# Casts of the first x ahead of its softmax, W1 in pairs of chunks over four PSUM banks, zero matmuls in the first softmax

## The chip, the cores and the metric

The kernel runs on one core of a Trainium2 chip. The metric is the device time of one execution in microseconds (us). Three runs of the kernel before took 282.36, 283.07 and 284.10 us. The engines are named as in the profile: PE is TensorE's matmul side and PEld its weight loads, DVE is VectorE, ACT is ScalarE, POOL is GpSimd, SP is SyncE, which here only issues DMAs.

## What is computed

The program is a cross attention between a sequence and a small state, followed by a two-layer network with SiLU. There are B = 8 blocks, H = 8 heads, S = 512 positions, Ns = 32 state rows, D = 64.

```
scores  = scale * x @ state^T             # per block and head: 512 x 32
a       = exp(scores) / sum over the 32 state rows
xread   = a @ state                       # 512 x 64
a2      = exp(scores^T) / sum over the 512 positions
sread   = a2 @ x                          # 32 x 64
tokens  = [xread; sread], heads side by side   # 8 * 544 rows of 512
h       = tokens @ w_in                   # 512 -> 2048
out     = (h * sigmoid(h)) @ w_out        # 2048 -> 512, float32
```

The reference subtracts the row maximum in each softmax; the kernel does not.

## The kernel before, in words

**The weights of a block.** For a block, `xread @ w_in` is `a @ (state @ w_in)`. So the kernel first makes `W1 = state @ w_in`, with the state laid out block-diagonally in `sbd`, and then multiplies it by the softmax `a`. W1 has four chunks of 512 columns. `w1_m` (line 231) computes one chunk with 8 matmuls of 64 rows by 32 columns into a pair of PSUM banks, `w1_e` (line 244) casts both banks to bf16 into the tile `W1`, and `W1x` (line 358) does the two for one chunk.

**The steps of a block.** `load_x` and `cast_x` (line 106) bring in x and cast it to bf16. `st_T` (115) transposes the state, `x_T` and `x_Te` (125, 132) transpose x and copy it out of PSUM, `sc` (136) makes the scores, `ex` (148) the exponentials on ACT. `norm_s` (158) sums rows and takes reciprocals on DVE, `norm_m` (163) multiplies, on POOL or DVE, and gives `an`. `a_T` (175) transposes `an` into PSUM and copies it to `aT`. `sread_m`, `sread_n`, `sread_t` (186, 211, 221) make the state read and put its transpose into `xsT`. `g1` (250) is the first layer for one of 16 tiles of 128 hidden columns: two matmuls into bank `h0` or `h1`, in turn, and a SiLU on ACT. `g2` (276) is one matmul of the second layer, `o_e` (295) copies a finished tile of 128 rows of output out of PSUM on DVE and stores it.

**The stages.** The first softmax (lines 331 to 343) takes the four 128-row pairs of heads of block 0 one after the other. Block 0's layers follow, with block 1's attention between them (lines 377 to 442). Then comes a transition (445 to 475). From line 504 on the work is in *phases*: `phase(k, fill)` (477) runs the 64 `g2` steps of block k (four output tiles of 16 steps, banks `o0` and `o1` in turn), and after a step it runs what `fill` lists for that step: the rest of the attention of block n = k + 1, its W1 and its `g1`, and the first part of the attention of block k + 2. `phase(1, ...)` runs only tiles 2 and 3, that is steps 32 to 63. Phases 2 to 6 come from one loop (514 to 528). Phase 7 and the state rows (`g_s`) end the program.

**What sets the order.** The schedule is manual: each engine runs its instructions in the order in which the program writes them, and semaphores are waited for where tiles or PSUM banks demand it. So a wait holds up all that is behind it on that engine. PSUM has eight banks: `o0`, `o1`, `w0`, `w1`, `h0`, `h1`, `a0`, `a1`. ACT loads one function table at a time, for exp or for SiLU; a load is an instruction of its own. `warm` (302) issues zero matmuls. `gate` (93) holds back a load of x by a small write of DVE.

Of the kernel before, what the change touches and what calls it, by code (L numbers as in the profile page):

```python
# [19 lines left out]
def kernel(  # L20
# [53 lines left out]
    def bf(name):  # L74
        return bank[name][:].bitcast(BF16)
# [30 lines left out]
    def cast_x(b, eng, kts=(0, 1, 2, 3)):  # L106
        for kt in kts:
            for h in range(2):
                cp(
                    eng,  # L110
                    x_n[b % 2][:, kt, :, h, :],
                    x_f[b % 2][:, kt, h, :].rearrange("p (c d) -> p c d", c=4),
                )

    def st_T(b, bk, e0, e1):
        v = bf(bk)[:, 0:128]
        nc.tensor.transpose(v, st_nat[:, b, :], ident[:])  # L117
        for half, e in ((0, e0), (1, e1)):
            cp(
                e,  # L120
                sbd[ds(64 * half, 64), b, :, half, :],
                v[ds(64 * half, 64)].rearrange("p (ns kt) -> p kt ns", kt=KT),
            )
# [12 lines left out]
    def sc(b, kt, bk):  # L136
        v = bank[bk][:].rearrange("p (k c e) -> p k c e", k=2, c=4)
        for c in range(4):
            nc.tensor.matmul(  # L139
                v[:, kt % 2, c, :],  # L140
                xT[b % 2][:, kt, c, :],
                sbd[:, b, kt, :, :],
                start=True,
                stop=True,
                skip_group_check=True,
            )

    def ex(b, kt, n, bk):
        v = bank[bk][:].rearrange("p (k q s) -> p k q s", k=2, q=8)
        nc.scalar.activation(  # L150
            en[b % 2][:, :, :, ds(kt, n), :].rearrange("p c h k s -> p k (c h) s"),
            v[:, ds(kt % 2, n)],
            func=EXP,
            bias=0.0,
            scale=SCALE,
        )
# [18 lines left out]
    def a_T(b, bks):  # L175
        n = 2 // len(bks)
        for i, (bk, e) in enumerate(bks):
            v = bf(bk).rearrange("p (h c t) -> p h c t", h=2, c=4)
            for half in range(n):
                for c in range(4):  # L180
                    nc.tensor.transpose(  # L181
                        v[:, half, c, :], an[b % 2][:, c, i * n + half, :, :], ident[:]
                    )
            cp(e, aT[b % 2][:, ds(i * n, n)], v[:, ds(0, n)])

    def sread_m(b, bk):
        v = bank[bk]
        for half in range(2):
            for c in range(4):
                for kt in range(KT):  # L190
                    nc.tensor.matmul(  # L191
                        v[ds(32 * kt, 32), ds(D * half, D)],
                        en[b % 2][:, c, half, kt, :],
                        x_n[b % 2][:, kt, c, half, :],
                        start=(c == 0),
                        stop=(c == 3),
                        skip_group_check=True,
                        tile_position=(0, 32 * kt),
                    )
        for half in range(2):  # L200
            for c in range(4):
                nc.tensor.matmul(
                    v[:, ds(128 + half, 1)],
                    en[b % 2][:, c, half, :, :],
                    ones[:],
                    start=(c == 0),
                    stop=(c == 3),
                    skip_group_check=True,
                )

    def sread_n(b, bk):
        v = bank[bk]
        nc.vector.reciprocal(srec[:], v[:, 128:130])
        nc.vector.tensor_tensor(
            sr[:],
            v[:, 0:128].rearrange("p (h d) -> p h d", h=2),
            srec[:].unsqueeze(2).to_broadcast([128, 2, D]),
            op=MULT,
        )
# [30 lines left out]
    def g1(b, ft):  # L250
        bk = bank[f"h{hctr[0] % 2}"]
        hctr[0] += 1
        if b < B:
            for half in range(2):
                nc.tensor.matmul(  # L255
                    bk[:],
                    W1[b % 2][:, half, ds(128 * ft, 128)],
                    aT[b % 2][:, half, :, :],
                    start=(half == 0),
                    stop=(half == 1),  # L260
                    skip_group_check=True,
                )
            nc.scalar.activation(g[b % 2][:, ft, :], bk[:], func=SILU, bias=0.0)  # L263
        else:
            for kt in range(KT):
                nc.tensor.matmul(  # L266
                    bk[:, 0:256],
                    w_in_sb[:, kt, ds(128 * ft, 128)],
                    xsT[:, kt, :, :, :],
                    start=(kt == 0),  # L270
                    stop=(kt == KT - 1),
                    skip_group_check=True,
                )
            nc.scalar.activation(g_s[:, ft, :], bk[:, 0:256], func=SILU, bias=0.0)  # L274

    def g2(b, tt, ft, bk, cols=(0, 512)):
        src = g[b % 2] if b < B else g_s
        c0, c1 = cols
        nc.tensor.matmul(  # L279
            bank[bk][:, c0:c1],  # L280
            src[:, ft, ds(128 * tt, 128)],
            w_out_sb[:, ft, c0:c1],
            start=(ft == 0),
            stop=(ft == 15),
            skip_group_check=True,
        )
# [8 lines left out]
    def o_e(b, tt, bk, eng="dve", q=None, cols=(0, 512)):  # L295
        t = o_sb[octr[0] % 4]
        octr[0] += 1
        c0, c1 = cols
        cp(eng, t[:, c0:c1], bank[bk][:, c0:c1])
        (q or nc.sync).dma_start(o_dst(b, tt, c0, c1), t[:, c0:c1])  # L300
# [8 lines left out]
    with tc.manual_schedule():  # L309
# [20 lines left out]

        XB = ("o0", "o1", "w0", "w1")
        SB = ("h0", "h1", "a0", "a1")
        st_T(0, "a1", "act", "dve")
        for i in range(5):
            if i < 4:
                cast_x(0, "dve", (i,))
                x_T(0, i, XB[i])
                x_Te(0, i, 1, XB[i], "act")
            if i > 0:
                sc(0, i - 1, SB[i - 1])  # L340
                ex(0, i - 1, 1, SB[i - 1])
                norm_s(0, i - 1, 1)
                norm_m(0, "dve", i - 1, 1)
        nc.scalar.preload_act_table(SILU)
        a_T(0, (("a0", "dve"), ("a1", "act")))
        w1_m(0, 0, ("w0", "w1"))
        w1_e(0, 0, ("w0", "w1"), ("dve", "act"))
# [10 lines left out]
        def W1x(b, j, bks, engs):  # L358
            w1_m(b, j, bks)
            w1_e(b, j, bks, engs)  # L360

        def exps(b):
            ex(b, 0, 2, "a0")
            ex(b, 2, 2, "a1")
            norm_s(b)
            norm_m(b, "pool")
# [78 lines left out]
        for ft in range(10):  # L445
# [5 lines left out]
            if ft == 7:  # L451
                scs(2, 0)
                scs(2, 1)
        exps(2)
        g1(1, 12)
        g1(1, 13)
        g2(1, 0, 10, "o0")
        g2(1, 0, 11, "o0")
        for ft in range(12):
            g2(1, 1, ft, "o1")  # L460
            if ft % 3 == 1:
                W1x(2, ft // 3, ("w0", "w1"), ("dve", "dve"))
            if ft == 5:
                sread_m(1, "a1")
                sread_n(1, "a1")
            if ft == 10:
                sread_t(1, "a1", "dve")
        cast_x(3, "pool")
        for ft in range(12, 16):
            g2(1, 0, ft, "o0")  # L470
            g2(1, 1, ft, "o1")
            if ft < 14:
                g1(1, ft + 2)
        o_e(1, 0, "o0")
        o_e(1, 1, "o1")

# [9 lines left out]
        def add(fill, step, *fs):  # L486
            fill.setdefault(int(step), []).extend(fs)

        def L(f, *a):
            return lambda: f(*a)  # L490

        def att_tail(fill, b, s_m, s_t, s_a):
            add(fill, s_m, L(sread_m, b, "a1"), L(sread_n, b, "a1"))
            add(fill, s_t, L(sread_t, b, "a1", "dve"))
            add(fill, s_a, L(a_T, b, (("a0", "dve"),)))
# [6 lines left out]
            add(fill, s1 + 2, L(scs, b, 1))  # L502

        fill = {}
        add(fill, 34, L(a_T, 2, (("a0", "dve"),)))
        for i in range(16):
            add(fill, 36 + 1.7 * i, L(g1, 2, i))
        add(fill, 38, L(sread_m, 2, "a1"), L(sread_n, 2, "a1"))
# [2 lines left out]
        phase(1, fill, (2, 3))  # L511


        for k in range(2, 7):
            n = k + 1
            fill = {}
            exps(n)
            if k + 2 < B:
                load_x(k + 2, nc.sync)
                cast_x(k + 2, "pool")  # L520
            for j in range(4):
                add(fill, 3 + 3 * j, L(W1x, n, j, ("w0", "w1"), ("dve", "dve")))
            att_tail(fill, n, 15, 25, 21)
            for i in range(16):
                add(fill, 25 + 2.3 * i, L(g1, n, i))
            if k + 2 < B:
                att_head(fill, k + 2, 42, 56)
            phase(k, fill)


        fill = {}
# [42 lines left out]
```

## Time and profile before

| what | value |
|---|---|
| runs | 282.36, 283.07, 284.10 us |
| profiled execution, its own time | 283.27 us |
| its span | 281.5 us |
| PE busy | 237.8 us (84%) |
| ACT busy | 120.1 us (43%) |
| DVE busy | 103.0 us (37%) |
| POOL busy | 43.8 us (16%) |
| mean DMA rate | 78 GB/s |

The span is the stretch between the first and the last instruction of the profiled execution; 1.77 us of its time lie outside it. An instruction's line is that of the helper that issued it, so most groups are told apart by the tiles they write: `ps_o`, `ps_w`, `ps_h`, `ps_a` are the PSUM banks. "idle before" is the time in which the engine stood still just before a group, with what released it. The busy time of a group of matmuls includes the tail of the last one, so the pace of a stream is read from one start to the next. PEclk is the clock granted to TensorE, as a share of 2.4 GHz.

### The profile page before, as it was taken

What the parts mean: (1) busy time and instruction counts of PE and PEld (TensorE: products, weight loads), DVE (VectorE), ACT (ScalarE), POOL (GpSimd) and SP (SyncE); (2) the same over time, 40 slices, a digit from 0 to 9 for tenths busy, and PEclk for the clock granted to TensorE, in tenths of its full rate; (3) what the DMA queues carried; (4) which work ended last, traced back from release to release, by engine and by line L of the source; (5) the groups of instructions that cost most, each with busy time, mean ns of one, the idle gap of its engine ahead of it and who ended that gap; (6) DMA issues with size and microseconds to landing.
All of it is one profiled execution on the core that took longest, in us unless ns stands there. A gap on an engine that the chain in (4) does not pass through costs nothing.

```text
span 281.5 us, 4371 instructions
## 1 busy us (share of the span) xinstructions
PE 237.8 (84%) x1777; PEld 112.8 (40%) x1810; DVE 103.0 (37%) x194; ACT 120.1 (43%) x194; POOL 43.8 (16%) x81
## 2 busy tenths in 40 slices
PE   4359979996889778996989778996989698999994
PEld 3223343342245324541435324541445234456643
DVE  3452215725533274226613273225603472000110
ACT  2353574566136604552075504562075505643301
POOL 5631202123300060002300060002300010000000
PEclk9999997999899979997799979998899979999999
DMA  5999800750020231006111231116010001110112
GB/s 170 188 202 204 175 2 0 239 212 1 0 77 37 71 119 40 37 37 186 38 39 40 68 118 40 38 40 186 37 41 37 37 2 45 66 40 37 40 75 76
DMA packets 19828, 22.07 MB, mean 78 GB/s; under 512 B 3040, under 2 KB 15584, under 8 KB 19808
## 3 DMA queue, kind: packets, MB, share of 16 engines
q1 hardware_dynamic: 12576, 16.39, 17.5%
q0 software_dynamic: 6128, 4.42, 10.5%
q10 hardware_dynamic: 1104, 0.98, 1.1%
q8 instruction: 14, 0.23, 0.3%
q14 instruction: 6, 0.05, 0.1%
HBM read 17.30 MB, written 8.91 MB: 93 GB/s over the span
## 4 chain that ended last, share of the span: by engine, by line
PE 71%; ACT 11%; DVE 10%; issue 5%; DMA 1%; ACTq 0%; POOL 0%; DVEq 0%
PE ps_o L279 33%; PE ps_h L255 19%; PE ps_w L234 4%; DVE W L79 3%; DVE rs L160 3%; ACT L150 3%; ACT en L150 3%; PE ps_w L279 3%; PE ps_h L266 2%; ACT g L263 2%; PE ps_a L128 2%; ACT L263 1%; PE ps_a L181 1%; DMA st_f<-in_state_dram 1%; PE ps_a L191 1%
## 5 line engine op out<-in xcount | busy, mean ns | idle before, releaser
L279 PE MATMUL ps_o<-w_out_sb,g 128*128 128x512 bf16 x458 | 137.4, 395 | 4.1 <-issue 2.2
L263 ACT ACTIVATE g<-ps_h 128x512 bf16<-128x512 f32 x128 | 75.4, 597 | 60.3 <-PE ps_h L255 56.5
L255 PE MATMUL ps_h<-aT,W 128*128 128x512 bf16 x246 | 74.8, 387 | 5.6 <-ACT g L263 3.6
L279 PEld LDWEIGHTS <-g 128*128 128x128 bf16 x512 | 47.6, 100 | 58.2 <-issue 14.8
L79 DVE COPY o_sb<-ps_o 128x512 f32<-128x512 f32 x30 | 20.5, 688 | 72.7 <-PE ps_o L279 72.7
L255 PEld LDWEIGHTS <-W 128*128 128x128 bf16 x256 | 24.7, 99 | 33.8 <-issue 7.7
L165 POOL TENSOR_TENSOR an<-en,rs 128x1024 bf16<-128x1024 bf16 x7 | 13.4, 1911 | 144.8 <-DVE rs L161 144.8
L79 DVE CAST W<-ps_w 128x512 bf16<-128x512 f32 x49 | 31.2, 678 | 12.5 <-PE ps_w L234 12.5
L263 ACT ACT_TABLE_LOAD x7 | 9.0, 1283 | 60.7 <-PE ps_h L255 60.6
L234 PE MATMUL ps_w<-w_in_sb,sbd 64*32 64x512 bf16 x200 | 17.6, 488 | 16.8 <-DVE W L79 16.6
L81 POOL CAST x_n<-x_f 128x256 bf16<-128x256 f32 x52 | 18.5, 407 | 25.1 <-DMA x_f<-in_x_dram 13.5
L234 PEld LDWEIGHTS <-sbd 64*32 64x32 bf16 x256 | 5.9, 92 | 39.5 <-issue 39.3
L160 DVE TENSOR_REDUCE rs<-en 128x32 f32<-128x1024 bf16 (+1 forms) x11 | 10.2, 929 | 25.0 <-ACT en L150 25.0
L128 PEld LDWEIGHTS <-x_n 128*128 128x128 bf16 x128 | 8.7, 102 | 9.4 <-DVE x_n L79 6.4
L79 DVE COPY xT<-ps_a 128x1024 bf16<-128x1024 bf16 x13 | 8.9, 691 | 9.5 <-PE ps_a L128 9.5
L79 DVE COPY sbd<-ps_a 64x128 bf16<-64x128 bf16 x15 | 4.3, 288 | 19.8 <-PE ps_a L117 16.8
L274 ACT ACTIVATE g_s<-ps_h 128x256 bf16<-128x256 f32 x16 | 6.1, 384 | 11.8 <-PE ps_h L266 11.8
L279 PE MATMUL ps_w<-w_out_sb,g 128*128 128x512 bf16 x31 | 10.2, 412 | 0.1
L266 PE MATMUL ps_h<-xsT,w_in_sb 128*128 128x256 bf16 x64 | 9.6, 273 | 0.0
L150 ACT ACT_TABLE_LOAD x7 | 9.0, 1283 | 0.1
L150 ACT ACTIVATE en<-ps_a 128x512 bf16<-128x512 f32 (+1 forms) x16 | 8.4, 568 | 0.3 <-PE ps_a L139 0.2
L128 PE MATMUL ps_a<-ident,x_n 128*128 128x128 bf16 x112 | 8.3, 219 | 0.0
(56 smaller groups left out, 122.7 us busy)
## 6 DMA issues: line engine op xcount, KB each, us to landing
out_dram<-o_sb SPq DMA_DIRECT2D x32, 256.0 KB, 2.3
x_f<-in_x_dram SPq DMA_DIRECT2D x7, 1024.0 KB, 6.4
w_in_sb<-in_moe_w_in_dram POOLq DMA_DIRECT2D x4, 512.0 KB, 11.4
w_out_sb<-in_moe_w_out_dram POOLq DMA_DIRECT2D x4, 512.0 KB, 13.2
x_f<-in_x_dram SPq DMA_DIRECT2D x2, 256.0 KB, 3.2
x_f<-in_x_dram ACTq DMA_DIRECT2D x2, 256.0 KB, 4.0
out_dram<-o_sb ACTq DMA_DIRECT2D x1, 256.0 KB, 2.5
st_nat<-in_state_dram POOLq DMA_DIRECT2D x7, 32.0 KB, 11.1
```

The source lines that it names most:

```text
L79: nc.vector.tensor_copy(dst, src)
L81: nc.gpsimd.tensor_copy(dst, src)
L128: nc.tensor.transpose(v[:, kt % 2, c, :], x_n[b % 2][:, kt, c, :, :], ident[:])
L150: nc.scalar.activation(en[b % 2][:, :, :, ds(kt, n), :].rearrange("p c h k s -> p k (c h) s"), v[:, ds(kt % 2, n)], func=EXP, bias=0.0, sc ...
L160: nc.vector.tensor_reduce(v, en[b % 2][:, :, :, ds(kt, n), :], axis=AX, op=ADD)
L165: e.tensor_tensor(an[b % 2][:, :, :, ds(kt, n), :].rearrange("p c h k s -> p (c h) k s"), en[b % 2][:, :, :, ds(kt, n), :].rearrange("p c ...
L234: nc.tensor.matmul(bank[bks[half]][ds(32 * kt, 32), :], sbd[ds(64 * half, 64), b, kt, half, :], w_in_sb[ds(64 * half, 64), kt, ds(512 * j, ...
L255: nc.tensor.matmul(bk[:], W1[b % 2][:, half, ds(128 * ft, 128)], aT[b % 2][:, half, :, :], start=(half == 0), stop=(half == 1), skip_group ...
L263: nc.scalar.activation(g[b % 2][:, ft, :], bk[:], func=SILU, bias=0.0)
L266: nc.tensor.matmul(bk[:, 0:256], w_in_sb[:, kt, ds(128 * ft, 128)], xsT[:, kt, :, :, :], start=(kt == 0), stop=(kt == KT - 1), skip_group_ ...
L274: nc.scalar.activation(g_s[:, ft, :], bk[:, 0:256], func=SILU, bias=0.0)
L279: nc.tensor.matmul(bank[bk][:, c0:c1], src[:, ft, ds(128 * tt, 128)], w_out_sb[:, ft, c0:c1], start=(ft == 0), stop=(ft == 15), skip_group ...
```

## The change

Four edits. (1) In the first softmax all eight casts of x come ahead of the loop, on DVE; the second of the two copies of the state transpose goes from DVE to ACT; 4, 4 and 14 zero matmuls are added. (2) In the transition the four W1 chunks of block 2 stand at other places, and the row sums and the multiplication (`norm_s`, `norm_m`) behind two of the chunks. (3) In phases 2 to 6 a new function `W1p` makes two chunks at a time, one into `w0`, `w1`, the other into `h0`, `h1`; the first pair stands at the start of the phase, ahead of `norm_s`, the second after step 18. (4) The copy of `aT` for blocks 2 to 7 goes from DVE to ACT, `a_T` stands at step 29 instead of 21, `sread` at 18 and 30 instead of 15 and 25, `g1` at 32 + 1.9 i instead of 25 + 2.3 i, the head of block k + 2 at 40 instead of 42.

```diff
--- before.py
+++ after.py
@@ -330,18 +330,22 @@
 
         XB = ("o0", "o1", "w0", "w1")
         SB = ("h0", "h1", "a0", "a1")
-        st_T(0, "a1", "act", "dve")
+        st_T(0, "a1", "act", "act")
+        warm(4, "h0")
+        cast_x(0, "dve", (0, 1, 2, 3))
         for i in range(5):
             if i < 4:
-                cast_x(0, "dve", (i,))
                 x_T(0, i, XB[i])
                 x_Te(0, i, 1, XB[i], "act")
             if i > 0:
                 sc(0, i - 1, SB[i - 1])
+                if i == 1:
+                    warm(4, "a1")
                 ex(0, i - 1, 1, SB[i - 1])
                 norm_s(0, i - 1, 1)
                 norm_m(0, "dve", i - 1, 1)
         nc.scalar.preload_act_table(SILU)
+        warm(14, "o0")
         a_T(0, (("a0", "dve"), ("a1", "act")))
         w1_m(0, 0, ("w0", "w1"))
         w1_e(0, 0, ("w0", "w1"), ("dve", "act"))
@@ -451,19 +455,24 @@
             if ft == 7:
                 scs(2, 0)
                 scs(2, 1)
-        exps(2)
+        ex(2, 0, 2, "a0")
+        ex(2, 2, 2, "a1")
         g1(1, 12)
         g1(1, 13)
         g2(1, 0, 10, "o0")
+        W1x(2, 0, ("w0", "w1"), ("dve", "dve"))
         g2(1, 0, 11, "o0")
         for ft in range(12):
             g2(1, 1, ft, "o1")
-            if ft % 3 == 1:
-                W1x(2, ft // 3, ("w0", "w1"), ("dve", "dve"))
-            if ft == 5:
+            if ft == 3:
+                W1x(2, 1, ("w0", "w1"), ("dve", "dve"))
+                norm_s(2)
+                norm_m(2, "pool")
                 sread_m(1, "a1")
+            if ft == 8:
                 sread_n(1, "a1")
-            if ft == 10:
+                W1x(2, 2, ("w0", "w1"), ("dve", "dve"))
+            if ft == 11:
                 sread_t(1, "a1", "dve")
         cast_x(3, "pool")
         for ft in range(12, 16):
@@ -471,6 +480,8 @@
             g2(1, 1, ft, "o1")
             if ft < 14:
                 g1(1, ft + 2)
+            if ft == 13:
+                W1x(2, 3, ("w0", "w1"), ("dve", "dve"))
         o_e(1, 0, "o0")
         o_e(1, 1, "o1")
 
@@ -502,7 +513,7 @@
             add(fill, s1 + 2, L(scs, b, 1))
 
         fill = {}
-        add(fill, 34, L(a_T, 2, (("a0", "dve"),)))
+        add(fill, 34, L(a_T, 2, (("a0", "act"),)))
         for i in range(16):
             add(fill, 36 + 1.7 * i, L(g1, 2, i))
         add(fill, 38, L(sread_m, 2, "a1"), L(sread_n, 2, "a1"))
@@ -511,20 +522,32 @@
         phase(1, fill, (2, 3))
 
 
+        WP = (("w0", "w1"), ("h0", "h1"))
+
+        def W1p(b, i):
+            for j in range(2):
+                w1_m(b, 2 * i + j, WP[j])
+            for j in range(2):
+                w1_e(b, 2 * i + j, WP[j], ("dve", "dve"))
+
         for k in range(2, 7):
             n = k + 1
             fill = {}
-            exps(n)
+            ex(n, 0, 2, "a0")
+            ex(n, 2, 2, "a1")
+            W1p(n, 0)
+            norm_s(n)
+            norm_m(n, "pool")
             if k + 2 < B:
                 load_x(k + 2, nc.sync)
                 cast_x(k + 2, "pool")
-            for j in range(4):
-                add(fill, 3 + 3 * j, L(W1x, n, j, ("w0", "w1"), ("dve", "dve")))
-            att_tail(fill, n, 15, 25, 21)
+            add(fill, 18, L(W1p, n, 1), L(sread_m, n, "a1"), L(sread_n, n, "a1"))
+            add(fill, 29, L(a_T, n, (("a0", "act"),)))
+            add(fill, 30, L(sread_t, n, "a1", "dve"))
             for i in range(16):
-                add(fill, 25 + 2.3 * i, L(g1, n, i))
+                add(fill, 32 + 1.9 * i, L(g1, n, i))
             if k + 2 < B:
-                att_head(fill, k + 2, 42, 56)
+                att_head(fill, k + 2, 40, 56)
             phase(k, fill)
 
 
```

Three places show what this does to the order of instructions. The first is DVE at the start of a phase (phase 2, block 3: `W_82` is its W1, `en_74` its exponentials, `rs_78` its row sums, `o_sb` output tiles). A piece of the difference, - before and + now:

```order
+L79 CAST W_82<-ps_w_97 128x512
+L79 CAST W_82<-ps_w_98 128x512
+L79 CAST W_82<-ps_h_99 128x512
+L79 CAST W_82<-ps_h_100 128x512
 L160 TENSOR_REDUCE rs_78<-en_74 128x32
 L161 RECIPROCAL rs_78<-rs_78 128x32
+L79 COPY o_sb_91<-ps_o_95 128x512
 L79 CAST W_82<-ps_w_97 128x512
 L79 CAST W_82<-ps_w_98 128x512
```

The casts of the first two chunks now stand ahead of the row sums, from four banks, and the first output tile of the phase is copied before the second pair of chunks.

The second place is ACT between the exponentials and the first SiLUs of the same block, the kernel as changed (`aT_80` is the transposed softmax, `g_84` the SiLU's output). A piece of the difference:

```order
+L150 ACT_TABLE_LOAD
+L150 ACTIVATE en_74<-ps_a_101 128x2x8x32
+L150 ACTIVATE en_74<-ps_a_102 128x2x8x32
+L83 ACTIVATE aT_80<-ps_a_101 128x1024
 L263 ACT_TABLE_LOAD
 L263 ACTIVATE g_84<-ps_h_99 128x512
```

The copy of `aT` has become the last thing that ACT does before it loads the SiLU table; before, DVE did it.

The third place is DVE in the first softmax (`x_f_67` is x as loaded, `x_n_69` its bf16 form, `an_75` the softmax):

```order
-L79 COPY sbd<-ps_a_102 64x4x32
-L79 CAST x_n_69<-x_f_67 128x4x64 x4
+L79 CAST x_n_69<-x_f_67 128x4x64 x8
 L160 TENSOR_REDUCE rs_77<-en_73 128x8
 L161 RECIPROCAL rs_77<-rs_77 128x8
 L165 TENSOR_TENSOR an_75<-en_73,rs_77 128x8x32
-L79 CAST x_n_69<-x_f_67 128x4x64 x2
```

The casts of the third and fourth pair of heads stood behind the row sums of the first and second; now no cast waits for a row sum.

## Rows read from the trace of the kernel before

**Rows 1.** Page, part 4: the chain that ended last, share of the span by engine.
```profile
PE 71%; ACT 11%; DVE 10%; issue 5%; DMA 1%; ACTq 0%; POOL 0%; DVEq 0%
```

**Rows 2.** Timeline, start of phase 4: start us, us, engine, line, operation [idle before].
```profile
158.99 0.41 PE L234 MATMUL ps_w<-w_in_sb,sbd 64*32 64x512 bf16 x8
159.33 0.82 PE L279 MATMUL ps_o<-w_out_sb,g 128*128 128x512 bf16 x3
...
160.52 1.22 DVE L160 TENSOR_REDUCE rs<-en 128x32 f32<-128x1024 bf16 x1 [1.60 <-ACT en L150]
...
162.05 1.22 DVE L79 CAST W<-ps_w 128x512 bf16<-128x512 f32 x2
162.30 1.91 POOL L165 TENSOR_TENSOR an<-en,rs 128x1024 bf16<-128x1024 bf16 x1 [25.56 <-DVE rs L161]
...
163.32 0.41 PE L234 MATMUL ps_w<-w_in_sb,sbd 64*32 64x512 bf16 x7 [0.22 <-DVE W L79]
```

**Rows 3.** Windows: length, busy (x) PE, PEld, DVE, ACT, POOL, PEclk, DMA, GB/s.
```profile
165.00:167.50 2.50, 2.05 (x17) 0.58 (x17) 1.35 (x3) 0.00 (x0) 1.47 (x5) 0.50 0.01 5
...
250.00:276.00 26.00, 25.84 (x160) 15.71 (x161) 3.46 (x5) 6.74 (x17) 0.00 (x0) 1.00 0.14 51
```

**Rows 4.** Timeline, the rest of phase 4.
```profile
168.66 0.42 PE L191 MATMUL ps_a<-x_n,en 128*32 128x64 bf16 x32
...
169.44 1.24 PE L279 MATMUL ps_o<-w_out_sb,g 128*128 128x512 bf16 x5
...
170.52 0.61 PE L181 MATMUL ps_a<-ident,an 128*128 128x128 bf16 x8
...
170.97 1.03 PE L279 MATMUL ps_o<-w_out_sb,g 128*128 128x512 bf16 x4
171.17 0.69 DVE L79 COPY aT<-ps_a 128x1024 bf16<-128x1024 bf16 x1 [0.67 <-PE ps_a L181]
...
171.91 0.59 PE L255 MATMUL ps_h<-aT,W 128*128 128x512 bf16 x2
...
174.53 0.59 PE L255 MATMUL ps_h<-aT,W 128*128 128x512 bf16 x2 [0.73 <-ACT g L263]
...
188.46 1.89 PE L279 MATMUL ps_o<-w_out_sb,g 128*128 128x512 bf16 x8
```

**Rows 5.** Timeline, an ACT copy of the size of `aT`, in block 0's stage.
```profile
36.92 1.02 ACT L83 ACTIVATE xT<-ps_a 128x1024 bf16<-128x1024 bf16 x1 [0.24 <-PE ps_a L128]
```

**Rows 6.** Timeline, the transition.
```profile
63.99 1.02 PE L279 MATMUL ps_o<-w_out_sb,g 128*128 128x512 bf16 x4
...
76.93 1.29 DVE L79 COPY o_sb<-ps_o 128x512 f32<-128x512 f32 x2 [1.53 <-PE ps_o L279]
...
79.71 1.24 PE L255 MATMUL ps_h<-aT,W 128*128 128x512 bf16 x4 [0.35 <-DVE aT L79]
```

**Rows 7.** Timeline, the first softmax.
```profile
6.10 1.04 PE L128 MATMUL ps_o<-ident,x_n 128*128 128x128 bf16 x8 [1.44 <-DVE x_n L79]
...
10.59 0.60 ACT L83 ACTIVATE xT<-ps_w 128x512 bf16<-128x512 bf16 x1 [2.38 <-PE ps_w L128]
...
13.08 0.61 PE L128 MATMUL ps_w<-ident,x_n 128*128 128x128 bf16 x4 [2.31 <-DVE x_n L79]
...
14.81 0.38 ACT L150 ACTIVATE en<-ps_a 128x256 bf16<-128x256 f32 x1 [0.21 <-PE ps_a L139]
...
16.84 1.03 PE L181 MATMUL ps_a<-ident,an 128*128 128x128 bf16 x8 [2.07 <-DVE an L165]
```

**Rows 8.** Windows of PE alone: length, busy (x), PEclk, DMA share, GB/s.
```profile
28.00:29.00 1.00, 1.00 (x7) 1.00 2.15 150
...
31.00:32.00 1.00, 1.00 (x7) 1.00 1.09 385
```

**Rows 9.** Timeline, block 1's x arrives and is transposed.
```profile
33.61 1.71 DVE L79 CAST x_n<-x_f 128x256 bf16<-128x256 f32 x4 [5.82 <-DMA x_f<-in_x_dram]
...
35.83 1.06 PE L128 MATMUL ps_a<-ident,x_n 128*128 128x128 bf16 x16
```

## The prediction, made before the change was run

> **What bounds the kernel now.** I read the page's chain first: 71% of the span is PE's, 21% ACT's and DVE's [rows 1]. So PE sets the time, except in places where it waits, and the question is where. The timeline answers that, one phase being enough because phases 2 to 6 come from one loop. Phase 4 starts four `g2` steps before its first W1 chunk, at 158.13 (158.99 less 4 x 0.216; five steps take 1.08 from 169.44 to 170.52) [rows 2, 4]. It ends at 189.32, four steps into the row at 188.46 [rows 4]: 31.19 us. The reader is to see two things in it. First, after one chunk and three steps PE stops near 160 and makes its next whole chunk only from 163.32, because `w0`, `w1` are still full: their casts run at 162.05, behind the row sums, which stand ahead of them on DVE and wait for the exponentials [rows 2]. Second, after that wait the granted clock is 0.50, the level of 1.2 GHz, in the stretch from 165.0 to 167.5 [rows 3], so chunks and steps run at half pace. From 163.32 to 168.66 PE does three chunks and nine steps, at full pace 3 x 0.34 + 9 x 0.216 = 2.96 us, in 5.34 [rows 2, 4]: 2.4 us lost to a second wait for casts and to the clock. From 174.53 to the end PE runs without a break.
>
> **The phases (edit 3, with the steps and `aT` of edit 4).** I write out a new phase from its start, with durations of phase 4.
> - A pair of chunks is 2 x 0.34 = 0.68 (158.99 to 159.33 is one) [rows 2]. Nothing holds it: `w0`, `w1` are empty, and the last SiLU on `h1` ends about 0.2 after the phase's start, before the second chunk needs it at 0.34.
> - Steps 0 to 18: 19 x 0.216 = 4.10, so 4.78. The second pair needs the four casts of the first. DVE copies an output tile (0.69, as 1.29 for two) [rows 6], then casts two pairs of banks at 1.22 each [rows 2]: done at about 3.3. No wait. The pair ends at 5.46.
> - `sread_m` 0.78 (168.66 to 169.44) gives 6.24, steps 19 to 29 give 8.62. `a_T` needs `an`: row sums 1.22 and reciprocal from 3.3 to about 4.9, then POOL's 1.91 [rows 2], so 7.0. Slack 1.6.
> - `a_T` 0.45 (170.52 to 170.97) gives 9.07; three steps and the transpose of `sr` give 9.80 [rows 4]. The transpose needs `sr` at 9.29. DVE copies tile 0 (to 5.55), casts four banks (to 8.0) and scales (to 8.5): slack 0.8.
> - `g1` needs `aT`. DVE's copy began 0.65 after the start of `a_T` and took 0.69 [rows 4]; an ACT copy of the same size took 1.02 [rows 5]. So `aT` is there at 8.62 + 0.65 + 1.02 + 0.05 = 10.34, and PE waits **0.54**, which it did not before.
> - From the first `g1` to the third PE takes 2.62 (171.91 to 174.53), bound by ACT's load of the SiLU table, not by PE's own work [rows 4]. That stays: 12.96. One step less than before covers it.
> - The rest took 14.79 with 34 steps (174.53 to 189.32); now 28 are left: 14.79 - 1.30 = 13.49. `g1` comes every 1.9 steps; two matmuls and two steps are 0.86, as in most of the old stretch, so the SiLUs keep up.
>
> The new phase is 26.45, 4.74 less; five of them make **23.7**. Bounds: if both waits behind step 29 vanished in full, a further 0.54 each, 26.4; if the clock falls there (a rival), 10 less.
>
> DMAs: the load of x for block k + 2 is issued from SP where it was, behind the last tile's store. POOL's casts of it stand behind `norm_m`, which ends later in the phase by some 0.9 us, but they are used only at step 42, far behind.
>
> **The transition (edit 2).** From 63.99 to the first `g1` of block 2 at 79.71 is 15.72 [rows 6]. PE's work in it is 27 steps (5.83), four chunks (1.36), two `g1` (0.86), `sread` with its transpose (0.86) and `a_T` (0.45): 9.36. With chunks 0 and 1 cast ahead of the row sums, DVE is busy nearly throughout from 64.6: eight casts in pairs of 1.22 to 1.29, row sums 1.5, the scaling and copy of `sr` 0.9, then the first output tile 0.69 [rows 2, 6], done at about 73.7. The waits left are some 0.3 for the casts of chunk 0, 0.45 for `sr`, 1.2 at step 32 for that tile, and 0.85 for `aT` from ACT: 2.8. So 9.36 + 2.8 = 12.2 and the gain is **3.6**. These waits lie close together; if the clock falls to its lower level there the gain is 1.9 or less. I keep 3.6 and take 1.6 as the lower end.
>
> **The first softmax (edit 1).** The transposes of the fourth pair of heads start at 13.08, having waited for its cast, and `a_T` follows 3.76 later at 16.84 [rows 7]. With all casts ahead, a pair of heads advances at ACT's pace, a copy of 0.60 and an exponential of 0.38 [rows 7]. If the first transposes still start at 6.10, the fourth start at about 6.10 + 3 x 1.0 = 9.1 and `a_T` at 12.8: 4.0 earlier. The second state copy on ACT (0.3 or less, a half of 0.60 by size) precedes the first transposes' copy and hides behind the casts. The zero matmuls cost nothing: at the pace of `a_T`'s eight, 1.03 in all, the last fourteen take 1.8, and PE's idle time ahead of `a_T` is 2.07 [rows 7].
>
> What of the 4.0 reaches the end depends on block 1's x. Its casts start when it lands, at 33.61, and its transposes at 35.83, hardly later than the casts allow [rows 9]. Its load is held back by `gate`, which moves with PE, to a time when more of the weights are still on their way. Beside the weights the two move 150 GB/s together, alone x moves 385 [rows 8]. So the load takes longer: if it gains nothing from its earlier issue, the term is 0; if it shares without loss, 4.0. Nothing in the trace decides; I take **2.0**.
>
> The Trainium skill (DMA: Bandwidth & Descriptors, section "SWDGE vs HWDGE vs iDMA") says that transfers issued from POOL and those from SP use different queues in each DMA engine, and that the engine serves its queues in turn. By that rule x gets about half of the 150 GB/s and lands no earlier than now, so the first softmax would give 0 and the time would be 256.0. The trace agrees so far as the joint rate is the lower one; one such stretch of 1 us is all that it shows.
>
> **The sum.** 2.0 + 3.6 + 23.7 = 29.3. The profiled execution took 283.27, 0.2 above the median of the runs shown, 283.07: 283.27 - 29.3 = **254.0 us**.
>
> **The rivals.**
> - *The clock falls behind step 29* (0.14). The 0.54 for `aT` and the 1.1 or so of the table load now lie within 3.2 us of each other, with 1.5 us of matmuls between. For it: a pause near 160 was followed by 0.50 [rows 3]. Against it: that pause was above 3 us, and the old wait of 0.73 at 174.53 was followed by unbroken work at full pace [rows 4]. Each fall costs at most the 2.4 us found above, say 2.0; in five phases 10: 264.
> - *The pause only moves* (0.05): the change does not do what it says, because the second chunk's bank `h1` comes free only when ACT is through, and the exponentials follow the SiLUs there. If PE waited for them, to about 2.6 after the phase's start, 2.3 would go in each phase: 265.5. Against it: the bank needs only the SiLU, which stands ahead of the table load and the exponentials.
> - *The clock falls and stays down, and the kernel is slower* (0.02). The same place, but TensorE does not come back to 2.4 GHz in the dense rest of the phase. 13.5 us at half clock add 13.5 per phase, 67 in all: 321. It decides from about 12 us at the lower level in each phase (29.3 / 5 is 5.9 us lost). Against it: after the pause of phase 4 the pace was full again by 169.44 [rows 4], and from 250 to 276 PE is busy for 25.84 of 26 us at a clock of 1.00 [rows 3], so density alone lowers nothing.
> - *The chains' slack is used up* (0.05): DVE or POOL runs later than I wrote, so that `sr` or `an` is late. Every 0.5 us beyond the slack of 0.8 or 1.6 costs 2.5 in five phases; 1 us gives 259.
>
> **The numbers.** My forecast has 0.74; the rivals 0.14, 0.05, 0.02 and 0.05. From the sum's bounds: the best is 4.0 + 3.6 + 26.4 = 34.0, 249; the worst without a rival 0 + 1.6 + 23.7 = 25.3, 258. The first rival reaches 264, and the range takes in most of it: 248 to 263. About 1% is what a measurement of this kernel tells from no change. All cases but the third rival are over 1% faster: 0.97 faster, 0.01 within, 0.02 slower.
>
> **What would show it.** In the changed profile the distance from one load of the exp table to the next should be 26 to 27 us in phases 2 to 5; no PE wait near the start of a phase; all eight casts of the W1 pairs without a PE wait on them; a wait of about 0.5 for `aT` from ACT and one of about 1 at the third `g1`; a granted clock of 1.00 throughout phases 2 to 6. Block 1's casts should start between 30 and 33, and the first `g1` of block 2 some 5 to 6 us earlier than 79.71. I am wrong if a 0.50 stretch appears in the phases, if the pause comes back elsewhere, or if the weights' loads become the bound of the first 40 us.

## The result and the profile after

The changed kernel took 254.85 us, the median of four runs (254.44 to 255.27), against 283.13 for the kernel before beside it (282.36 to 284.1): a ratio of 0.900, 95% interval 0.897 to 0.903. The forecast was 254.0 in 248 to 263. The profiled run took 255.27; its span is 253.5, so 1.77 lie outside it, as before. From profiled run to profiled run the change gained 28.0 us, where 29.3 were forecast.

The page of the changed kernel first: span, busy times, the row of the granted clock over 40 slices of 6.3 us, and the chain that ended last.

```profile
span 253.5 us, 4473 instructions
...
PE 226.9 (90%) x1832; PEld 112.4 (44%) x1832; DVE 95.8 (38%) x187; ACT 126.4 (50%) x201; POOL 43.8 (17%) x81
...
PEclk9959989999999999999999999999999999999999
...
PE 77%; ACT 7%; DVE 6%; DMA 6%; issue 3%; ACTq 0%; DVEq 0%
```

PE now carries 77% of the chain where it had 71%, and ACT and DVE 13% where they had 21% [rows 1]. The share of DMA has grown from 1% to 6%, and the clock's row has its low slices near the start alone, in the third and the sixth. Both are taken up below.

To split the gain I take ACT's loads of the exp table, one at the head of every block's exponentials, as marks in both traces.

| from mark to mark | before | after | gain | forecast |
|---|---|---|---|---|
| start to the load at 63.53 / 64.07 | 63.53 | 64.07 | -0.54 | 2.0 |
| from there to 95.01 / 92.36 (transition, phase 1) | 31.48 | 28.29 | 3.19 | 3.6 |
| from there to 220.39 / 197.27 (phases 2 to 5) | 125.38 | 104.91 | 20.47 | 18.96 (4 x 4.74) |
| the rest (phase 6 and the end) | 62.88 | 58.00 | 4.88 | 4.74 |

The last row is the profiled time less the mark. So the phases gave 25.35 (23.7 forecast), the transition nearly its 3.6, and the first softmax cost a little where it should have given 2.0.

**A phase.** The timeline of the changed kernel, phase 2 (start us, us, engine, line, operation, idle before), which answers to [rows 2, 4]:

```profile
92.00 0.41 PE L234 MATMUL ps_w<-w_in_sb,sbd 64*32 64x512 bf16 x8
...
92.23 0.56 PE L234 MATMUL ps_h<-w_in_sb,sbd 64*32 64x512 bf16 x8
92.36 1.28 ACT L150 ACT_TABLE_LOAD   x1
...
92.72 1.28 DVE L79 CAST W<-ps_w 128x512 bf16<-128x512 f32 x2
...
92.73 4.28 PE L279 MATMUL ps_o<-w_out_sb,g 128*128 128x512 bf16 x19
...
93.92 1.28 DVE L79 CAST W<-ps_h 128x512 bf16<-128x512 f32 x2
95.11 1.21 DVE L160 TENSOR_REDUCE rs<-en 128x32 f32<-128x1024 bf16 x1
...
96.93 0.41 PE L234 MATMUL ps_w<-w_in_sb,sbd 64*32 64x512 bf16 x8
...
97.49 0.42 PE L191 MATMUL ps_a<-x_n,en 128*32 128x64 bf16 x32
...
100.42 0.61 PE L181 MATMUL ps_a<-ident,an 128*128 128x128 bf16 x8
...
101.13 1.02 ACT L83 ACTIVATE aT<-ps_a 128x1024 bf16<-128x1024 bf16 x1 [6.39 <-PE ps_a L181]
...
102.20 0.59 PE L255 MATMUL ps_h<-aT,W 128*128 128x512 bf16 x2 [0.47 <-ACT aT L83]
...
102.88 1.28 ACT L263 ACT_TABLE_LOAD   x1 [0.72 <-PE ps_h L255]
...
104.82 0.59 PE L255 MATMUL ps_h<-aT,W 128*128 128x512 bf16 x2 [0.94 <-ACT g L263]
...
118.55 1.28 ACT L150 ACT_TABLE_LOAD   x1
```

The reader is to see that no PE row of the phase before 102.20 carries an idle time. The pair of chunks at 92.00 goes straight into 19 steps, while DVE casts all four banks before it sums the rows. Only the two forecast waits are left: for `aT` at 102.20 and for the SiLU at 104.82. From one exp load to the next are 26.19 us. The clock behind those waits stays at 2.4 GHz, as the windows of the changed kernel show (length, busy (x) of PE, PEclk, DMA share, GB/s); the last row is more than three phases, the others belong to the next two readings and answer to [rows 8]:

```profile
12.00:13.00 1.00, 0.92 (x8) 0.50 1.44 185
21.00:22.00 1.00, 0.78 (x10) 1.00 1.24 207
27.00:28.00 1.00, 1.00 (x13) 1.00 1.15 243
30.00:31.00 1.00, 0.69 (x4) 1.00 1.32 275
32.00:33.00 1.00, 0.00 (x0) 1.00 1.73 136
37.00:38.00 1.00, 1.00 (x3) 0.50 0.00 0
45.00:46.00 1.00, 0.80 (x10) 1.00 0.00 0
118.00:200.00 82.00, 77.76 (x660) 1.00 0.26 81
```

**The start and the transition.** The timeline of the changed kernel there, which answers to [rows 6, 7, 9]:

```profile
9.47 0.94 PE L304 MATMUL ps_o<-zeros 128*128 128x128 bf16 x14
12.08 1.03 PE L181 MATMUL ps_a<-ident,an 128*128 128x128 bf16 x8 [1.66 <-DVE an L165]
...
33.55 1.72 DVE L79 CAST x_n<-x_f 128x256 bf16<-128x256 f32 x4 [11.07 <-DMA x_f<-in_x_dram]
...
34.52 0.40 PE L128 MATMUL ps_a<-ident,x_n 128*128 128x128 bf16 x4 [3.83 <-DVE x_n L79]
...
64.54 0.38 PE L279 MATMUL ps_o<-w_out_sb,g 128*128 128x512 bf16 x1
...
74.63 0.81 PE L279 MATMUL ps_o<-w_out_sb,g 128*128 128x512 bf16 x3 [1.03 <-DVE o_sb L79]
...
77.06 0.59 PE L255 MATMUL ps_h<-aT,W 128*128 128x512 bf16 x2 [0.74 <-ACT aT L83]
```

`a_T` of block 0 starts at 12.08, 4.76 earlier than at 16.84 [rows 7]. But block 1's x is cast from 33.55, where it was 33.61 [rows 9]: its load was released at 22.42 instead of 27.73 and took 11.1 us where it had taken 5.9. PE comes to the transposes of x 3.83 early and waits there, and behind that wait the clock stands at 0.50, the level of 1.2 GHz, from 36 to 39. The transition runs from 64.54 to 77.06, 12.52 us, against 15.72 [rows 6] and a forecast of 12.2.

### The profile page after: what moved, and what is told of

It is laid out like the page before. It is cut to its first block, busy times and chain, and to the rows that moved or that the text cites. A ratio compares the mean times of both kernels' runs of the same rounds, so it can differ in the third digit from the quotient of the medians.

```text
span 253.5 us, 4473 instructions
## 1 busy us (share of the span) xinstructions
PE 226.9 (90%) x1832; PEld 112.4 (44%) x1832; DVE 95.8 (38%) x187; ACT 126.4 (50%) x201; POOL 43.8 (17%) x81
## 4 chain that ended last, share of the span: by engine, by line
PE 77%; ACT 7%; DVE 6%; DMA 6%; issue 3%; ACTq 0%; DVEq 0%
PE ps_o L279 39%; PE ps_h L255 21%; DMA x_f<-in_x_dram 6%; PE ps_h L266 3%; PE ps_a L128 3%; ACT aT L83 2%; PE ps_w L279 2%; PE ps_w L234 2%; ACT g L263 2%; PE ps_a L181 2%; DVE W L79 2%; DVE rs L160 2%; PE ps_a L139 1%; ACT L263 1%; DVE x_n L79 1%
## 5 line engine op out<-in xcount | busy, mean ns | idle before, releaser
L279 PE MATMUL ps_o<-w_out_sb,g 128*128 128x512 bf16 x480 | 133.4, 381 | 1.1 <-DVE o_sb L79 1.0
L255 PE MATMUL ps_h<-aT,W 128*128 128x512 bf16 x256 | 76.8, 385 | 9.5 <-ACT g L263 4.7
L83 ACT ACTIVATE aT<-ps_a 128x1024 bf16<-128x1024 bf16 (+1 forms) x8 | 7.3, 918 | 37.8 <-PE ps_a L181 37.8
L79 DVE CAST W<-ps_w 128x512 bf16<-128x512 f32 x29 | 18.7, 684 | 7.8 <-PE ps_w L234 7.8
L79 DVE CAST W<-ps_h 128x512 bf16<-128x512 f32 x20 | 12.8, 681 | 0.0
L128 PE MATMUL ps_a<-ident,x_n 128*128 128x128 bf16 x112 | 8.9, 225 | 4.2 <-DVE x_n L79 4.2
L79 DVE CAST x_n<-x_f 128x256 bf16<-128x256 f32 x12 | 3.9, 383 | 13.9 <-DMA x_f<-in_x_dram 13.9
## 6 DMA issues: line engine op xcount, KB each, us to landing
out_dram<-o_sb SPq DMA_DIRECT2D x32, 256.0 KB, 2.4
x_f<-in_x_dram SPq DMA_DIRECT2D x2, 256.0 KB, 3.0
x_f<-in_x_dram ACTq DMA_DIRECT2D x2, 256.0 KB, 3.8
out_dram<-o_sb ACTq DMA_DIRECT2D x1, 256.0 KB, 2.5
```

Of the source, the lines that this page charges most:

```text
L79: nc.vector.tensor_copy(dst, src)
L83: nc.scalar.activation(dst, src, func=COPY, bias=0.0)
L128: nc.tensor.transpose(v[:, kt % 2, c, :], x_n[b % 2][:, kt, c, :, :], ident[:])
L255: nc.tensor.matmul(bk[:], W1[b % 2][:, half, ds(128 * ft, 128)], aT[b % 2][:, half, :, :], start=(half == 0), stop=(half == 1), skip_group ...
L279: nc.tensor.matmul(bank[bk][:, c0:c1], src[:, ft, ds(128 * tt, 128)], w_out_sb[:, ft, c0:c1], start=(ft == 0), stop=(ft == 15), skip_group ...
```

## The experiments

Ten kernels were run. "After" is the changed kernel, and each edit is made to it. Ratios are to the kernel before on the same chip, with their 95% intervals; after has 0.900. The medians of the kernel before beside them lie between 282.80 and 284.02 us, so a difference to after in us is good to about 1 us; where the trace has the length of a phase, that is the firmer number. After's phases are 26.23 long on average (104.91 / 4).

**1. The first softmax as before.** Edit 1 is taken back.

```diff
-        st_T(0, "a1", "act", "act")
-        warm(4, "h0")
-        cast_x(0, "dve", (0, 1, 2, 3))
+        st_T(0, "a1", "act", "dve")
         for i in range(5):
             if i < 4:
+                cast_x(0, "dve", (i,))
...
-                if i == 1:
-                    warm(4, "a1")
...
-        warm(14, "o0")
```

> The kernel as changed, but with the first softmax as it was before (casts inside the loop, second state copy on DVE, no zero matmuls). Theory A: up to about 33.5 us the DMAs are the bound, since block 1's x lands at 33.5 whether its load is issued at 22.4 or at 27.8; so edit 1 is worth nothing: 254.3, between 253.8 and 255.4, with the DVE casts of block 1 again starting at 33 to 34 and no PE wait of 3.8 us in front of them. Rival B: edit 1 gave the predicted 2.0 and something else took it back: 256.5 to 257.

256.36 us (254.3 to 256.85), ratio 0.904 (0.900 to 0.908). That lies between the two expectations, and its runs show what it goes with: those with a mean granted clock of 1.00 and 0.993 took 254.3 and 254.77, the four at 0.985 or 0.986 took 256.28 to 256.85. The timeline of this kernel:

```profile
33.67 1.71 DVE L79 CAST x_n<-x_f 128x256 bf16<-128x256 f32 x4 [6.95 <-DMA x_f<-in_x_dram]
```

and, of PE,

```profile
34.77 0.39 PE L128 MATMUL ps_a<-ident,x_n 128*128 128x128 bf16 x4
```

The x lands where it lands in after, with its load released 4.3 us later, and PE arrives at the transposes just in time for it, 0.25 behind after. So nearly all of the 4.8 us that edit 1 gains in front is spent in the wait for x. What is left between the medians, 1.5, goes with the clock later on: the profiled run of this kernel (256.85) loads the exp table for block 1 at 38.89, ahead of after's 40.22, and for block 2 at 65.68, behind after's 64.07. In between it was at 1.2 GHz from 43 to 49.5, where after's was not (its row 45 to 46 above, against this one of PE).

```profile
45.00:46.00 1.00, 1.00 (x10) 0.50 0.00 0
```

**2. Block 1's x loaded early.** Its gate and load stand right behind the casts of block 0.

```diff
         cast_x(0, "dve", (0, 1, 2, 3))
+        gate(1)
+        load_x(1, nc.sync)
...
-        gate(1)
-        load_x(1, nc.sync)
         cast_x(1, "dve", (0, 1))
```

> The kernel as changed, with the gate and the load of block 1's x moved to right behind the casts of block 0's x, so at about 7 us instead of 22.4. Theory A: the wait of 3.8 us ahead of block 1's transposes and the low clock behind it go; PE does not wait for the weights, which land some 3 us later than now but are used later still: 249 to 251. Rival B: the DMAs are the bound through the weights too, so PE waits for w_in or w_out instead of x: 253.5 to 256, with PE or DVE waits on them between 12 and 30 us.

250.50 us (250.06 to 251.22), ratio 0.884 (0.881 to 0.887): 4.4 us less than after, as Theory A had it. The timeline of this kernel, DVE and PE:

```profile
22.70 0.89 DVE L79 CAST x_n<-x_f 128x256 bf16<-128x256 f32 x4
```

```profile
30.82 1.06 PE L128 MATMUL ps_a<-ident,x_n 128*128 128x128 bf16 x16
```

Neither row has an idle time: the x, issued at 7.12, is there before DVE asks for it, and PE transposes it at 30.82 instead of 34.52. PE never waits for weights; the one new wait for a load is 1.02 at 14.74, for a tile of the state.

**3. Both: the old first softmax with the early load.** Experiment 1, with the gate and the load behind the casts of the second pair of heads.

```diff
                 cast_x(0, "dve", (i,))
+                if i == 1:
+                    gate(1)
+                    load_x(1, nc.sync)
```

> Both: the first softmax as it was before, and the load of block 1's x issued behind the second pair of casts (about 6.5 us). Theory A: with the load out of the way the first softmax is the bound of the start, so this is slower than the early load with the new softmax by the 4 to 5 us that edit 1 takes off it: 253.5 to 255.5. Rival B (edit 1 is worthless of itself): the same time as the early load alone, within 1 us.

254.87 us (254.16 to 256.15), ratio 0.901 (0.897 to 0.905). All four corners are now there:

| | load late | load early |
|---|---|---|
| old first softmax | 256.4 | 254.9 |
| new first softmax (edit 1) | 254.9 | 250.5 |

With the early load edit 1 is worth 4.4, nearly the 4.76 by which `a_T` moved, as Theory A had it; with the late one 1.5, with overlapping intervals. The early load alone gains little too (1.5, also with overlapping intervals), because the old first softmax does not bring PE to x before it lands. The runs of this kernel fall apart by the clock as in experiment 1: 254.16 and 254.42 at 1.00, 256.07 and 256.15 at 0.986.

**4. Without the zero matmuls.** The three calls of `warm` are taken out of the first softmax.

```diff
-        warm(4, "h0")
...
-                    warm(4, "a1")
...
-        warm(14, "o0")
```

> The kernel as changed, without the 22 zero matmuls that it adds. Theory A: whatever they do to the clock up to 30 us is hidden by the wait for block 1's x: 254.9, within 0.6. Rival B: they keep the clock up in a place that counts: 256 or more.

255.40 us (254.5 to 256.76), ratio 0.902 (0.899 to 0.906): 0.5 more than after, with intervals that overlap. They cost nothing that can be measured, and no gain of theirs is shown; Theory A held.

**5. The SiLU table loaded early.** In phases 2 to 6 ACT loads the SiLU table right behind the exponentials, where it idles.

```diff
             ex(n, 2, 2, "a1")
+            nc.scalar.preload_act_table(SILU)
```

> The kernel as changed, with the SiLU table loaded right behind the exponentials in phases 2 to 6, and not at the first SiLU. Theory A: the 2.62 us from the first g1 to the third are the table's, so PE's wait of about 1 us there goes in each phase: 249.0 to 250.0. Rival B: the wait is for the first g1's own SiLU, or moves to aT: 254 to 255.

250.51 us (249.66 to 250.89), ratio 0.881 (0.876 to 0.887): 4.3 less than after, and half a microsecond above the range of Theory A. The timeline of this kernel, PE in phase 2:

```profile
103.10 0.59 PE L255 MATMUL ps_h<-aT,W 128*128 128x512 bf16 x2 [0.47 <-ACT aT L83]
...
104.61 0.59 PE L255 MATMUL ps_h<-aT,W 128*128 128x512 bf16 x2
```

From the first `g1` to the third are 1.51 us instead of 2.62, and the wait of 0.94 is gone, while the 0.47 for `aT` stays. The phase is 25.09 long (93.25 to 118.34), and phases 2 to 5 take 25.20 on average, 1.03 less than after's. So 1.11 of the 2.62 was the wait for the table load, and 1.51 is the pace that is left without it. What is missing from Theory A's gain lies in front of the phases: block 2's exp load stands at 64.97 here and at 64.07 in after.

**6. Two banks instead of four.** Both chunks of a pair go through `w0`, `w1`.

```diff
-        WP = (("w0", "w1"), ("h0", "h1"))
+        WP = (("w0", "w1"), ("w0", "w1"))
...
                 w1_m(b, 2 * i + j, WP[j])
-            for j in range(2):
                 w1_e(b, 2 * i + j, WP[j], ("dve", "dve"))
```

> The kernel as changed, with pairs of chunks still ahead of the row sums, but both chunks of a pair in w0 and w1, each cast behind its own matmuls. Theory A: four banks are needed; the second chunk of each pair waits for the casts of the first, 1.7 us at the phase's start and 1.3 after step 18: about 15 us more, 266 to 272. Rival B: it is the order ahead of the row sums alone that gives the gain: 254 to 257.

272.59 us (272.04 to 272.93), ratio 0.960 (0.955 to 0.964): 17.7 more than after, 3.5 per phase, and 0.6 above the range of Theory A. The timeline of this kernel, PE in phase 2:

```profile
93.96 0.37 PE L234 MATMUL ps_w<-w_in_sb,sbd 64*32 64x512 bf16 x1 [1.04 <-DVE W L79]
94.56 0.41 PE L234 MATMUL ps_w<-w_in_sb,sbd 64*32 64x512 bf16 x7 [0.23 <-DVE W L79]
...
100.92 0.41 PE L234 MATMUL ps_w<-w_in_sb,sbd 64*32 64x512 bf16 x7 [0.22 <-DVE W L79]
```

In both pairs the second chunk waits for the casts of the first, as in [rows 2]. The idle column alone shows 1.04 and 0.23, but from one chunk's start to the next whole one's (92.51 to 94.56) are 2.05, and in the second pair (99.10 to 100.92) 1.82, against 0.23 in after: 3.4 in all, which is the loss per phase (29.61 on average, for 26.23).

**7. Row sums first.** Four banks, but `norm_s` and `norm_m` stand ahead of the first pair.

```diff
+            norm_s(n)
+            norm_m(n, "pool")
             W1p(n, 0)
-            norm_s(n)
-            norm_m(n, "pool")
```

> The kernel as changed, with four banks, but the row sums and the multiplication ahead of the first pair of chunks, as before. Theory A: the casts of the first pair then end at about 6.7 us of the phase, and the second pair at 4.8 waits for them: 1.5 us in each phase, 261 to 263, up to 2 more for each phase in which the clock falls. Rival B: four banks alone give the gain: 254 to 256.

263.34 us (262.83 to 263.73), ratio 0.927 (0.923 to 0.932): 8.5 more than after, 1.7 per phase, and 0.3 above the range of Theory A. The timeline of this kernel, DVE:

```profile
94.21 1.22 DVE L160 TENSOR_REDUCE rs<-en 128x32 f32<-128x1024 bf16 x1 [2.03 <-ACT en L150]
...
95.73 1.22 DVE L79 CAST W<-ps_w 128x512 bf16<-128x512 f32 x2
```

and PE:

```profile
96.41 0.37 PE L234 MATMUL ps_w<-w_in_sb,sbd 64*32 64x512 bf16 x1
...
98.20 0.41 PE L234 MATMUL ps_h<-w_in_sb,sbd 64*32 64x512 bf16 x7 [0.23 <-DVE W L79]
```

DVE stands 2.03 idle for the exponentials with the casts queued behind the row sums, and the second pair then runs at the pace of the casts: 1.8 from its start to its last chunk, in after 0.23. Both halves of edit 3 are needed, the banks and the place ahead of the sums; the banks are worth twice as much. In experiments 6 and 7 the granted clock stayed 1.00 through the phases (windows from 94 to 240), so what they price is the waits alone. The old phase lost by waits and by 1.2 GHz behind them [rows 2, 3]; the fall of the clock came back in neither, and its share of the gain of 5.1 per phase was not measured by itself. Nor was a kernel run with the new steps of edit 4 alone.

**8. The points put together.** Experiments 2 and 5, and `a_T` at step 27 instead of 29.

```diff
-            add(fill, 29, L(a_T, n, (("a0", "act"),)))
+            add(fill, 27, L(a_T, n, (("a0", "act"),)))
```

> A candidate that should beat both: early load of block 1's x (250.5 measured), the SiLU table behind the exponentials (5.5 less), and a_T at step 27 instead of 29 in phases 2 to 6, so that the wait of 0.5 us for aT goes (2.4 less). Theory A: 242 to 244. Rival B, the gains share a wait: 246 to 249.

243.06 us (242.4 to 243.46), ratio 0.856 (0.852 to 0.860): it beats both kernels, after by 11.8, as Theory A had it. The timeline of this kernel, PE in phase 2:

```profile
96.65 0.59 PE L255 MATMUL ps_h<-aT,W 128*128 128x512 bf16 x2
...
98.16 0.59 PE L255 MATMUL ps_h<-aT,W 128*128 128x512 bf16 x2
```

No wait is left at the first or the third `g1`: `a_T` stands two steps earlier, and the steps behind it cover ACT's copy. The phase is 24.66 long (87.23 to 111.89).

**9. The old transition.** Edit 2 is taken back.

```diff
-        ex(2, 0, 2, "a0")
-        ex(2, 2, 2, "a1")
+        exps(2)
...
-            if ft == 3:
-                W1x(2, 1, ("w0", "w1"), ("dve", "dve"))
-                norm_s(2)
-                norm_m(2, "pool")
+            if ft % 3 == 1:
+                W1x(2, ft // 3, ("w0", "w1"), ("dve", "dve"))
...
```

> The kernel as changed, with the transition (edit 2) as it was before. Theory A: the transition gave 3.2 us (12.5 from the first step behind the SiLUs to block 2's first g1, against 15.7): 257.5 to 259. Rival B: part of those 3.2 comes with the phases or the first softmax: 255 to 256.5.

259.57 us (258.35 to 260.0), ratio 0.917 (0.912 to 0.921): edit 2 is worth 4.7, and the time is 0.6 above the range of Theory A. The timeline and a window of this kernel:

```profile
68.35 0.37 PE L234 MATMUL ps_w<-w_in_sb,sbd 64*32 64x512 bf16 x1 [2.04 <-DVE W L79]
```

```profile
70.00:73.00 3.00, 2.76 (x52) 0.50 0.00 0
```

The old order brings back a wait of 2.04 for a cast and behind it 1.2 GHz. The run at the highest mean clock, 0.987 as in after, took 258.35, 3.5 more than after's median; the others were at 0.971 to 0.974. By that one run about 3.5 of the 4.7 is the waits, and the rest goes with a lower clock.

**10. `aT` copied by DVE.** In phases 2 to 6, at step 29 as in after.

```diff
-            add(fill, 29, L(a_T, n, (("a0", "act"),)))
+            add(fill, 29, L(a_T, n, (("a0", "dve"),)))
```

> The kernel as changed, with aT in phases 2 to 6 copied by DVE and not by ACT, still at step 29. Theory A: DVE is free there and its copy is 0.33 shorter, so PE's wait of 0.5 shrinks to 0.2 and five phases give 1.6: 252.8 to 253.8. Rival B: DVE is behind with the casts of the second pair and the copy of sr, so aT comes later: 255 to 258.

253.02 us (252.7 to 253.18), ratio 0.894 (0.892 to 0.897): 1.8 less than after, as Theory A had it, with intervals that just touch. The timeline of this kernel, DVE and PE:

```profile
100.74 0.69 DVE L79 COPY aT<-ps_a 128x1024 bf16<-128x1024 bf16 x1 [0.78 <-PE ps_a L181]
```

```profile
101.49 0.59 PE L255 MATMUL ps_h<-aT,W 128*128 128x512 bf16 x2
```

The copy is 0.69 instead of 1.02 and the wait at the first `g1` is gone. The phase is 25.80 long (92.03 to 117.83), 0.39 less, 1.95 in five. So the move of this copy to ACT, a part of edit 4, is a loss of 1.8 to 1.95 within the gain.

## Why the prediction was right, and where it was not

**The phases: right, by the steps as written.** Counted from the first chunk at 92.00, the second pair ended at 5.49 (forecast 5.46), `a_T` began at 8.42 (8.62), the first `g1` at 10.20 (10.34), the third at 12.82 (12.96), and the exp loads are 26.19 apart (26.45). The wait for `aT` showed as 0.47 (0.54). The 0.2 comes from `sread_m`: I took 0.78 from a row at the end of the slow stretch of the old phase, and at full pace it is 0.56 (97.49 to 98.05). That the phases gave 25.35 and not 23.7 has a second cause: I measured the old phase on phase 4 alone (31.19), and the four from the marks average 31.35. Experiments 6 and 7 show the mechanism by putting back one cause at a time; 5 does the same for the table load and 10 for the copy of `aT`. The upper bound of 26.4 for this term took off only the 0.54 in each phase; with the wait at the third `g1` gone too it would have been larger, as experiment 8 shows with 24.77 per phase on average.

**The first rival did not happen.** The two waits behind step 29 lie 2.6 us apart, yet the clock stayed 1.00 from 118 to 200, and in the other phases too (92 to 118, 200 to 250). Nor did the second and the fourth: `h1` was free in time, and `sr` and `an` were not waited for.

**The transition: the size held.** 3.2 by the marks, 3.5 to 4.7 by experiment 9, against 3.6. The wait for the first output tile (1.03, forecast 1.2) and for `aT` (0.74, forecast 0.85) are there.

**The first softmax: the term that was mis-sized.** It was put at 2.0 between 0 and 4.0, and measured -0.54 from profile to profile. The step that failed is the choice between its bounds: "if it gains nothing from its earlier issue, the term is 0; if it shares without loss, 4.0. Nothing in the trace decides; I take 2.0." The front gained more than I wrote, 4.76 for 4.0, but x, issued 5.3 us earlier, landed at the same moment. The working of the lower bound misread its row: the window of 150 GB/s [rows 8] is not one of weights and x together. Of its 1071 packets 4 were x's, and 1047 were under 512 bytes. The DMA queues of the kernel before from 28 to 29, POOL's (q0) and SP's (q1): packets, MB, share of 16 engines:

```profile
q0 software_dynamic: 1067, 0.15, 213.4%
q1 hardware_dynamic: 4, 0.00, 1.3%
```

The same queues of the changed kernel, from 22.5 to 26 (no line for q1: not a packet) and from 27 to 28:

```profile
q0 software_dynamic: 732, 0.72, 123.9%
...
q0 software_dynamic: 119, 0.12, 70.9%
q1 hardware_dynamic: 119, 0.12, 43.8%
```

So x, issued at 22.53, moved nothing until 26.0, which took 3.5 of the 5.3 us, and from then on it shared packet for packet with the weights, at 243 GB/s together, against 207 before it joins. In experiment 2 its first packet also came some 4 us behind the issue, in the kernel before, with the weights nearly through, about 1; what holds it back is not shown. In before, after and experiments 1 to 3 alike nearly all traffic ends between 33 and 34: the bytes of that stretch are the same in each order, and in after x shares with the weights and the loads of the state to the end. What I did not ask is when x would have to be issued to be clear of that end; experiment 2 shows that 7 us is early enough and that PE does not miss the weights that then come later.

The Trainium skill (DMA: Bandwidth & Descriptors, section "SWDGE vs HWDGE vs iDMA") was cited for the end at 0: an engine that serves its queues in turn would let x land no earlier, which gave 256.0. The trace agrees on the landing, on the missing gain and on the turns (119 packets of each queue from 27 to 28), and not on the joint rate, which was above the 150 GB/s of that working.

The middle between two bounds was the wrong choice here for a plain reason: the loads are a chain of their own, with an end at 33 us that the edit does not move, and PE's chain joins it there. A gain in front of such a join counts only as far as the other chain has slack, and [rows 9] show that it had little: the transposes stand 2.22 behind the first cast, and after needed 0.97 for the same, so at most some 1.25 of the 4.76 could count. Even that went: behind the transposes PE was 0.35 ahead of before (its next step at 36.37 for 36.72), and at the next `g1` 0.69 behind (38.94 for 38.25), because that stretch of after ran at 1.2 GHz behind the 3.83 us wait. This is one profile of each kernel, and before had a low stretch of its own a little later (42 to 45.3). Two of the signs named in advance thus failed: the casts of block 1 began at 33.55 and not between 30 and 33, and the first `g1` of block 2 came 2.65 earlier and not 5 to 6.

**The offsetting.** The mis-sized terms are 2.5 too much in the first softmax, 0.4 too much in the transition and 1.7 too little in the phases. That they cancel in part, so that 254.0 lies within 1 us of 254.85, is luck; the phases, which carry most of the gain, are not.

## What to carry to other kernels

Where a bank or a buffer makes the fastest engine wait, look first at what stands ahead of the releasing instruction in its own queue: the place of the casts ahead of the row sums was worth 1.7 us per phase, the second pair of banks 3.5. When a stage is shortened in front of a join, find the other chain's end before counting the gain, and move that chain too: here two changes of 1.5 each alone made 5.9 together (experiments 1 to 3). After a gain, read the waits that are left by what they wait for, since a table load and a copy on the slower engine were worth another 1 us and 0.4 us a phase.

## What was not expected of the hardware

- **Loads beside each other.** The casting loads of the weights (issued by POOL) and the plain load of x (issued by SP) moved 243 GB/s together from 27 to 28, with the same number of packets each; the weights alone moved 207. From 30 to 31 it was 275, with 235 packets of x (0.24 MB) beside 234 of POOL's queue that moved only 0.03 MB. And x began 3.5 to 4 us behind its issue when the weights were in full flow.
- **The clock at the start.** The fourteen zero matmuls took 0.94 us, yet after the wait of 1.66 behind them the clock was 0.50 in the window from 12 to 13 and 1.00 again by 19 to 20; without them the time was the same within the noise. In experiment 4, without them, the row reads 1.00 from 12 to 20, yet the first four matmuls of the second layer there take 1.69 us (16.96 to 18.65), the pace of after at 0.50 (17.02 to 18.72) and half of the full one (four in 0.86). So near the start of a trace that row alone does not tell the pace; why is open.
- **The same kernel at two clocks.** In experiment 1 runs of one kernel on one chip differ by about 2 us with the mean granted clock, 1.00 or 0.985. The two profiles shown above differ in the same way: behind the waits at 39 to 45 us one was at 1.2 GHz and the other not. What decides it stays open, and a single profile of such a stretch is weak evidence.
